# Start and end of a token-mixing kernel rearranged: who copies chunk 0 out of PSUM, where chunk 1 is convolved, the order of the last two steps

## The chip, the cores and the metric

The kernel runs on one core of a Trainium2 chip. The metric is device time of one execution in microseconds (us). Engines are named as the profile names them: PE (TensorE, matrix products), DVE (VectorE), ACT (ScalarE), POOL (GpSimd), SP (SyncE). SP and POOL each feed a queue of transfers (DMA); what stands in a queue is issued strictly in order.

## The reference

Input `x` is 8 batches x 4224 tokens x 192 channels, fp32.

```python
w = softmax(weight)                       # 8 head groups x 7 taps
x = causal depthwise convolution(x, w)    # the 24 channels of a head group share their taps
theta = x @ w_theta                       # 192 x 192
zr, zi = x * cos(theta), x * sin(theta)
y = w_tok_r @ zr + w_tok_i @ zi           # along the tokens, 4224 x 4224 each
u = x + y
out = u + relu(u @ w_ch)                  # 192 x 192
```

The two products along the tokens are almost all of the arithmetic.

## The kernel before

**Tiles.** The 4224 tokens are cut in 33 chunks of 128, each made of 32 tokens from each quarter of the sequence. A row of a tile is a token; its 1536 columns are 8 batches x 192 channels. Output tokens are in 33 blocks of 128, taken in pairs (17 units). Data are fp16 for PE, sums fp32.

**Chunk.** `Chunk.__init__` loads the tokens (four transfers by POOL, L199, into `xw`) and copies the 16 tokens of history before each quarter out of the chunk before (four transfers by SP, L190, `xw<-xw`). `conv(j)` convolves half of the channels on PE with band matrices (L212, into PSUM tile `pc`) and `evacuate` copies the result as fp16 into `z` (L150 on DVE or L152 on ACT). `conv_batches(g)` (L237) does it for chunk 0 alone, by halves of the batches, with two copies each: one on ACT, one on DVE. `store` writes x to DRAM (L259, SP). `transpose` turns it on PE (`tp`, L166) and copies it to `uT`. `theta(g)` multiplies with w_theta (PE, `v`, L142) and takes cosine and sine as two Sin on ACT (L287), for half of the batches. `product` multiplies by x on DVE (L293); `sums` forms differences (L302).

**Step.** There are 58 steps, each for one unit of output blocks and the chunks that are at hand then: two in step 0, growing to 11. `load_w` loads token weights (POOL, L369) into one of two `st` buffers, `turn` transposes them on DVE in 32x32 squares (L382, `wt`), `wsum` forms sums of weights (L394). A pair of blocks needs seven products in place of eight (`runs`, a Strassen scheme); steps 0 and 1 use the plain eight. `mix` (L500) issues the matmuls (L513, into `y`) and inserts other work at given places; `give` (L448) adds a finished `y` to `pv` (DVE, L456; in the first round ACT copies, L454). Rounds one and two keep `pv` in DRAM (`part`, L526). In the last steps (53 to 57: 9, 7, 6, 4 and 2 chunks) `outputs` makes the result: `cast` of `pv` to fp16 (`ub`), `turn_u` (PE `tp`, then `uT`), `output` (PE `v` with w_ch, then DVE L546 and the store L551). The last step has a single block.

**Buffers.** PSUM: two for `pc`, `tp`, `v` (pool `mmps`), two for `y` (pool `yps`). `xw` and most `pv` share six buffers called "big"; `z` has eleven.

**Order.** Each engine executes in program order (`in_order`), so order in the source is order on the chip. At the start the source writes the order out by hand: chunk 0, then a loop over chunks 1 to 12 in which `between(n)` inserts up to n pairs of `y` matmuls whose chunks are ready. `idle(n)` issues n matmuls of zeros (`noise`, L671): eight in front of the taps' matmuls (`bp`, L705), the others in gaps of the start. `step_events` (L584) places the tasks of a step at times from 0 to 7, 7 being its end.

Of the kernel before, what the change touches and what calls it, by code (L numbers as in the profile page):

```python
# [10 lines left out]
ALU = mybir.AluOpType  # L11
F16 = mybir.dt.float16
# [4 lines left out]
def kernel(  # L17
# [70 lines left out]
    def dve(ins):  # L88
        return in_order("dve", ins)
# [34 lines left out]
    wth = constp.tile([P, 4, D], F16, name="wth")  # L124
    wch = constp.tile([P, 4, D], F16, name="wch")

    def channel_pieces(w):

        return ((slice(0, P), 0, w[0:P, :]), (slice(0, R), 1, w[P:D, :]),
                (slice(R, P), 2, w[0:R, :]), (slice(0, P), 3, w[R:D, :]))  # L130
# [27 lines left out]

        act(nc.scalar.dma_start(out=uT, in_=u, transpose=True))

    def transposed(uT, u, gs, by_dve=False):

        tp = banks("tp", F16)
        for g in gs:
            for k in range(6):
                pe(nc.tensor.transpose(  # L166
                    tp[:, g, k * P : (k + 1) * P],
                    u[:, g * GC + k * P : g * GC + (k + 1) * P], ident,
                ))
        g = slice(gs[0], gs[-1] + 1)  # L170
        evacuate(
            uT[:, :, :].rearrange("p (g k) s -> p g (k s)", g=NG)[:, g, :],
            tp[:, g, 0 : 6 * P], by_dve,
        )
# [4 lines left out]
    class Chunk:  # L179
# [21 lines left out]
                    in_=x[:, t0 : t0 + n, :].rearrange("b s d -> s b d"),  # L201
                )

        def conv(self, j):

            if j == 0:
                self.z = zpool.tile([P, 7, HN], F16, name="z", tag="z")
                self.x = self.z[:, T2 : T2 + 2, :].rearrange("p t n -> p (t n)")
            pc = banks("pc")
            for h in range(4):  # L210
                for half in range(2):
                    pe(nc.tensor.matmul(  # L212
                        pc[half * 2 * Q : (half + 1) * 2 * Q, h // 2,
                           h % 2 * B * G : (h % 2 + 1) * B * G],
                        lhsT=bands[:, 4 * j + h, :, :].rearrange("p a m -> p (a m)"),
                        rhs=self.xw[:, half, :, (4 * j + h) * G : (4 * j + h + 1) * G],
                        start=True, stop=True,
                    ))
            evacuate(
                self.x.rearrange("p (b d) -> p b d", d=D)[  # L220
                    :, :, 4 * j * G : 4 * (j + 1) * G
                ].rearrange("p b (i h g) -> p i h b g", i=2, h=2),
                pc[:, :, 0 : 2 * B * G].rearrange("p i (h b g) -> p i h b g", h=2, b=B),
                self.k == 1 or (self.k in (2, 3) and j == 1),
            )
            if j == 1:
                self.store()

        def conv_batches(self, g):

            if g == 0:
                self.z = zpool.tile([P, 7, HN], F16, name="z", tag="z")
                self.x = self.z[:, T2 : T2 + 2, :].rearrange("p t n -> p (t n)")
            pc = banks("pc")
            for h in range(H):
                for half in range(2):
                    pe(nc.tensor.matmul(  # L237
                        pc[half * 2 * Q : (half + 1) * 2 * Q, h // 4,
                           h % 4 * GB * G : (h % 4 + 1) * GB * G],
                        lhsT=bands[:, h, :, :].rearrange("p a m -> p (a m)"),  # L240
                        rhs=self.xw[:, half, g * GB : (g + 1) * GB, h * G : (h + 1) * G],
                        start=True, stop=True,
                    ))
            for i in range(2):
                evacuate(
                    self.x.rearrange("p (b d) -> p b d", d=D)[
                        :, g * GB : (g + 1) * GB, 4 * i * G : 4 * (i + 1) * G
                    ].rearrange("p b (h g) -> p h b g", h=4),
                    pc[:, i, 0 : 4 * GB * G].rearrange("p (h b g) -> p h b g", h=4, b=GB),
                    i == 1,  # L250
                )
            if g == NG - 1:
                self.store()
# [17 lines left out]
        def transpose_batches(self, g):  # L271
            if g == 0:
                self.xT = turned()
            transposed(self.xT, self.x, [g], True)

        def theta(self, g):
            v = channel_mix(self.xT[:, 6 * g : 6 * g + 6, :], wth).rearrange(
# [52 lines left out]
    class Step:  # L330


        def __init__(self, t):
# [18 lines left out]
                    self.ahead.append((i, 2 * NU - NW + 2 * (t % NU) if far else start[-1],  # L352
                                       (t // NU - 1 - far) % 2))
            self.plain = self.first and self.pair and self.n <= NP
            self.time = 0.324 * self.n * (8 if self.plain else 7 if self.pair else 4)
            self.st, self.w, self.xr, self.ub, self.uT, self.pv = {}, {}, {}, {}, {}, []

        def known(self, tb):
# [99 lines left out]
        def runs(self):  # L458


            if self.pair:
                return [
                    ("11", Z11, "c1", True, (0, 0, True)),
                    ("S1", T1, "c2", True, (1, 1, True)),
                    ("S2", T2, "c1", False, (0, 1, True)),
                    ("S4", Z22, "c2", False, (0, 1, False)),
                    ("S3", T3, "c1", False, (1, 1, False)),
                    ("12", Z21, "c3", True, (0, 0, False)),
                    ("22", T4, "c1", False, (1, 0, True)),
                ]  # L470
            return [
                ("11", Z11, "c1", True, (0, 1, True)),
                ("11", T1, "c2", True, None),
                ("12", Z21, "c1", False, (0, 0, True)),
                ("12", Z22, "c2", False, (0, 1, False)),
            ]
# [23 lines left out]
        def mix(self, events):  # L500
# [23 lines left out]
            if not self.final:  # L524
                for i, tb in enumerate(self.tbs):
                    nc.sync.dma_start(  # L526
                        out=part[(self.t // NU) % 2][tb, :, :], in_=self.pv[i]
                    )

        def cast(self, i, g):  # L530
            if g == 0:
                self.ub[i] = wk.tile([P, N], F16, name="ub", tag="ub", bufs=2)
                self.uT[i] = turned()
            cols = slice(g * GC, (g + 1) * GC)
            evacuate(self.ub[i][:, cols], self.pv[i][:, cols], self.t >= NSTEP - 2 and g == 0)

        def turn_u(self, i, g):
            transposed(self.uT[i], self.ub[i], [g])

        def cross_u(self, i):  # L540
            crossed(self.uT[i], self.ub[i])

        def output(self, i, g):
            u = self.pv[i][:, g * GC : (g + 1) * GC]
            ub = u.rearrange("p (k n) -> p k n", k=2)
            dve(nc.vector.scalar_tensor_tensor(  # L546
                out=ub, in0=channel_mix(self.uT[i][:, 6 * g : 6 * g + 6, :], wch), scalar=0.0, in1=ub,
                op0=ALU.max, op1=ALU.add,
            ))
            rows = slice(self.tbs[i] * P, (self.tbs[i] + 1) * P)  # L550
            nc.sync.dma_start(  # L551
                out=out[g * GB : (g + 1) * GB, rows, :].rearrange("b s d -> s b d"),
                in_=u.rearrange("p (b d) -> p b d", d=D),
            )

        def outputs(self):

            found = []
            for i in range(len(self.tbs)):
                if not self.late:  # L560
                    at = 1 if i or not self.pair else 0.9 - self.time / 7
# [13 lines left out]
            return found  # L575

    steps = [Step(t) for t in range(NSTEP)]
    NPS = max(s.t for s in steps if s.plain)
    outputs = [
        (sum(s.time for s in steps[: t + 1]) + at, f)  # L580
# [3 lines left out]
    def step_events(t):  # L584
        found = []
        s = steps[t]
        if t + 1 < NSTEP:
            found += steps[t + 1].w_tasks()
            found.append((1.6, steps[t + 1].load_rows))
            for i in steps[t + 1].adds:  # L590
                found.append((2 + 2 * i, lambda i=i: steps[t + 1].load_x(i)))
                found.append((3.6 + 2 * i, lambda i=i: steps[t + 1].add_x(i)))
# [106 lines left out]
    ))  # L699
    taps = constp.tile([KS, H], F16, name="taps")  # L700
    dve(nc.vector.tensor_tensor(out=taps, in0=wcol, in1=wsum[0:KS, :], op=ALU.mult))
    idle(8)
    bp = banks("bp")
    for q in range(Q):
        pe(nc.tensor.matmul(  # L705
# [31 lines left out]

    steps[0].load_rows()
    steps[0].load_w(1)
    load_chunk(2)  # L740
    steps[0].load_w(2)
    load_chunk(3)
    for m in (1, 2):
        steps[1].load_w(m)
    load_chunk(4)
    load_chunk(5)
    for g in range(NG):
        chunks[0].conv_batches(g)
    idle(2)
    for g in range(NG):  # L750
        chunks[0].transpose_batches(g)
    for i in range(1, NW + 2):
        ch = chunks.get(i) if i < NW else None
        old = chunks[i - 1] if i <= NW else None

        def between(n):
            left = more(n)
            if i < 3:
                idle(min(left, 2) if i == 1 else 0)

        if ch:
            ch.conv(0)
        between(2)
        if old:
            old.theta(0)
        ready[0] = i - 2
        between(1)
        if ch:
            ch.conv(1)
        between(2)  # L770
        if old:
            old.theta(1)
        if i in (1, 3):
            for name in ("11", "21"):
                steps[i // 2].turn(name)
        if i + 3 < NW:
            load_chunk(i + 3)
        between(1)
        if i == 1:
            for first in (Z11, Z21):  # L780
                old.product(first, slice(0, 1))
        if ch:
            ch.transpose()
        if i == 1:
            for first in (Z11, Z21):
                old.product(first, slice(1, 2))
        elif old:
            old.product(Z11)
        between(2)
        if i > 1 and old:  # L790
            old.product(Z21)
        if i in (1, 3):
            for name in ("12", "22"):
                steps[i // 2].turn(name)
        between(1)
        if old and start[i - 1] > NPS:
            old.sums(0)
# [38 lines left out]
```

## Time and profile before

| | us |
|---|---|
| median of three runs | 1437.17 (1436.29 to 1440.14) |
| the profiled execution | 1437.24 |
| its span (first to last instruction) | 1435.4 |
| PE busy | 1410.6 (98%) |
| DVE busy | 973.8 (68%) |
| POOL busy | 434.4 (30%) |
| ACT busy | 310.8 (22%) |

The profile is of one execution. "Busy" is time in which an engine executes; the issuing of transfers is not counted on SP. "Idle before, releaser" is the gap ahead of an instruction and what ended it. The chain of waits runs back from the last instruction and gives 90% of its length to PE. TensorE's granted clock had a mean of 0.999 of full speed.

### The profile page before, as it was taken

Reading aid. Unit: us, or ns where it says so; the run is one execution under the profiler, and the core shown is the slowest. Engines: PE = TensorE matmul, PEld = TensorE weight load, DVE = VectorE, ACT = ScalarE, POOL = GpSimd, SP = SyncE. Lnnn points to the kernel's source line nnn. Section 1 sums busy time; section 2 is a strip of 40 time slices with the busy share of each in tenths; the row PEclk is TensorE's granted clock in tenths of the full one; section 3 lists DMA queues with packets and bytes.
Section 4 is the critical chain, followed back from the end, with each engine's and each line's share of the span. In section 5 each row is a group of like instructions: output and inputs, shape, how many; then the busy total and the mean of one; then the engine's idle time right before and its main releaser. Section 6 shows DMA issues by size and latency. Waiting matters only on the chain.

```text
span 1435.4 us, 23761 instructions
## 1 busy us (share of the span) xinstructions
PE 1410.6 (98%) x9825; PEld 890.3 (62%) x9825; DVE 973.8 (68%) x1046; ACT 310.8 (22%) x374; POOL 434.4 (30%) x655
## 2 busy tenths in 40 slices
PE   8899999999999999999999999999999999999997
PEld 5556666666666666666666666666566666666665
DVE  6893554545548787866666657877777677767686
ACT  5951101111124254000000004435100110010133
POOL 8511211111233332532433343233324123213120
PEclk9999999999999999999999999999999999999999
DMA  9975766564699999898899989989999999999884
GB/s 187 241 162 134 147 122 131 97 151 91 145 232 227 232 237 234 214 258 176 227 242 223 236 149 247 235 194 258 257 212 205 218 205 217 204 195 199 167 204 146
DMA packets 272028, 281.98 MB, mean 196 GB/s; under 512 B 106672, under 2 KB 240176, under 8 KB 271920
## 3 DMA queue, kind: packets, MB, share of 16 engines
q0 software_dynamic: 162464, 92.15, 48.5%
q1 hardware_dynamic: 71824, 178.88, 35.2%
q10 hardware_dynamic: 37632, 9.44, 4.6%
q8 instruction: 77, 1.26, 0.4%
q14 instruction: 31, 0.25, 0.1%
HBM read 245.49 MB, written 108.13 MB: 246 GB/s over the span
## 4 chain that ended last, share of the span: by engine, by line
PE 90%; DMA 5%; DVE 2%; ACT 1%; POOL 1%; issue 1%; DVEq 0%; ACTq 0%; POOLq 0%; SPq 0%
PE y L513 81%; PE v L142 5%; DMA xw<-in_x_dram 2%; DMA st<-in_moe_w_tok_r_dram 2%; PE tp L166 1%; PE pc L212 1%; ACT z L287 1%; DVE wt L382 1%; POOL st L369 1%; DVE pv L456 1%; DVE pv L546 0%; POOL xw L199 0%; DMA xw<-xw 0%; DMA st<-in_moe_w_tok_i_dram 0%; DMA wsb<-in_weight_dram 0%
## 5 line engine op out<-in xcount | busy, mean ns | idle before, releaser
L513 PE MATMUL y<-z,wt 128*128 128x384 f16 x7668 | 1281.9, 326 | 4.9 <-DVE pv L456 3.7
L513 PEld LDWEIGHTS <-wt 128*128 128x128 f16 x7668 | 743.6, 98 | 481.9 <-issue 5.6
L456 DVE TENSOR_TENSOR pv<-y,pv 128x768 f32<-128x768 f32 x318 | 303.3, 954 | 321.4 <-PE y L513 281.3
L382 DVE STREAM_TRANSPOSE wt<-st 128x1408 f16<-128x1408 f16 (+7 forms) x224 | 327.4, 1465 | 50.1 <-PE y L513 36.2
L369 POOL DMA_DIRECT2D st<-in_moe_w_tok_r_dram x232 | 132.3, 578 | 459.8 <-DVE wt L382 448.7
L369 POOL DMA_DIRECT2D st<-in_moe_w_tok_i_dram x232 | 132.5, 579 | 407.0 <-DVE wt L382 398.3
L394 DVE TENSOR_TENSOR wt<-wt 128x1408 f16<-128x1408 f16 (+6 forms) x208 | 173.3, 833 | 40.2 <-PE y L513 38.0
L152 ACT ACTIVATE z<-pc 128x768 f16<-128x768 f32 (+1 forms) x62 | 47.5, 803 | 385.6 <-PE pc L212 381.3
L152 ACT ACTIVATE ub<-pv 128x768 f16<-128x768 f32 x63 | 50.2, 835 | 334.1 <-DVE pv L456 305.3
L454 ACT ACTIVATE pv<-y 128x768 f32<-128x768 f32 x66 | 53.7, 814 | 280.4 <-PE y L513 280.4
L142 PEld LDWEIGHTS <-uT 128*128 128x128 f16 x1056 | 91.2, 98 | 24.6 <-issue 8.0
L434 POOL TENSOR_TENSOR pv<-pv,xr 128x1536 f32<-128x1536 f32 x24 | 74.4, 3102 | 66.7 <-DVE pv L546 21.9
L199 POOL DMA_DIRECT2D xw<-in_x_dram x132 | 76.3, 587 | 26.3 <-ACT pv L454 5.2
L546 DVE SCALAR_TENSOR_TENSOR pv<-v,pv 128x768 f32<-128x768 f32 x66 | 62.9, 954 | 27.5 <-PE v L142 27.0
L302 DVE TENSOR_TENSOR z<-z 128x768 f16<-128x768 f16 x132 | 71.2, 553 | 2.2
L287 ACT ACTIVATE z<-v,half_pi 128x768 f16<-128x768 f32 x66 | 59.7, 904 | 57.8 <-PE v L142 57.1
L152 ACT ACTIVATE uT<-tp 128x1536 f16<-128x1536 f16 (+1 forms) x47 | 56.7, 1209 | 56.9 <-PE tp L166 56.9
L293 DVE TENSOR_TENSOR z<-z 128x1536 f16<-128x1536 f16 (+1 forms) x68 | 60.6, 926 | 4.2 <-ACT z L287 4.2
L142 PE MATMUL v<-wth,uT 128*128 128x192 f16 x528 | 55.0, 248 | 2.7 <-ACT z L287 2.2
L142 PE MATMUL v<-wch,uT 128*128 128x192 f16 x528 | 54.2, 246 | 2.1 <-DVE pv L546 1.2
L287 ACT ACTIVATE z<-v 128x768 f16<-128x768 f32 x66 | 53.3, 807 | 0.0
L212 PE MATMUL pc<-xw,bands 96*64 96x192 f16 x512 | 30.5, 253 | 4.0 <-DMA xw<-xw 3.3
(45 smaller groups left out, 145.0 us busy)
## 6 DMA issues: line engine op xcount, KB each, us to landing
part<-pv SPq DMA_DIRECT2D x79, 768.0 KB, 4.2
pv<-part SPq DMA_DIRECT2D x79, 768.0 KB, 6.0
out_dram<-pv SPq DMA_DIRECT2D x66, 384.0 KB, 4.6
st<-in_moe_w_tok_r_dram POOLq DMA_DIRECT2D x136, 176.0 KB, 5.8
st<-in_moe_w_tok_i_dram POOLq DMA_DIRECT2D x136, 176.0 KB, 5.3
xs<-z SPq DMA_DIRECT2D x132, 96.0 KB, 5.0
xw<-in_x_dram POOLq DMA_DIRECT2D x121, 96.0 KB, 6.4
xr<-xs SPq DMA_DIRECT2D x24, 384.0 KB, 4.5
```

Of the source, the lines that this page charges most:

```text
L142: pe(nc.tensor.matmul(v[:, k, b * D : (b + 1) * D], lhsT=tT[:, 3 * k + b + i, :], rhs=w[:, 2 * b + i, :], start=(i == 0), stop=(i == 1),))
L152: act(nc.scalar.activation(out=out, in_=in_, func=AT.Copy))
L199: nc.gpsimd.dma_start(out=self.xw[lo : lo + n, h, :, :], in_=x[:, t0 : t0 + n, :].rearrange("b s d -> s b d"),)
L287: act(nc.scalar.activation(**args))
L302: dve(nc.vector.tensor_tensor(out=z[:, o, :], in0=z[:, a, :], in1=z[:, b, :], op=ALU.subtract))
L369: pool(nc.gpsimd.dma_start(out=st[a * Q : (a + 1) * Q, 0:nb, :, 0:n] .rearrange("i r bt s -> i (r bt) s"), in_=w[self.tbs[0] * P : (self.t ...
L382: dve(nc.vector.transpose(self.w[name][:, 0 : self.n, :, :], self.st[int(name[1])][:, int(name[0]) - 1, :, 0 : self.n * Q] .rearrange("p b ...
L394: dve(nc.vector.tensor_tensor(out=self.w[name][:, 0 : self.n, :, :], in0=self.w[a][:, 0 : self.n, :, :], in1=self.w[b][:, 0 : self.n, :, : ...
L434: ins = pool(nc.gpsimd.tensor_tensor(out=self.pv[i], in0=self.pv[i], in1=self.xr[i], op=ALU.add))
L456: dve(nc.vector.tensor_tensor(out=o, in0=yv, in1=o, op=ALU.add))
L513: pe(nc.tensor.matmul(y[cn][:, q, 0:BH], lhsT=self.w[wn][:, c, :, :].rearrange("p bt i -> p (bt i)"), rhs=chunks[k].z[:, zn, q * BH : (q + ...
L546: dve(nc.vector.scalar_tensor_tensor(out=ub, in0=channel_mix(self.uT[i][:, 6 * g : 6 * g + 6, :], wch), scalar=0.0, in1=ub, op0=ALU.max, o ...
```

## The change

- `conv_batches`: the two copies of a half of chunk 0 are cut by batches, no longer by channels; each reads both PSUM banks.
- `transpose_batches`: the second half of `uT` of chunk 0 is copied by ACT in place of DVE.
- The start is written out for chunks 0 and 1: theta(0) and theta(1) of chunk 0 follow each other with only the convolutions of chunk 1 between them. These are put in the PSUM buffers of `y` (`loose`). All other `idle` matmuls of the start go, except two; in front of the taps there are 12 in place of 8.
- The second weight load of step 0 is issued before the load of chunk 2. The four `turn`s of step 0 come in the order 11, 12, 21, 22 (before: 11, 21, 12, 22), and the second digit tells the `st` buffer that is read (1: w_tok_r, 2: w_tok_i).
- In the loop, one pair of `y` matmuls is moved from after the transposition to before theta(1).
- `load_rows` (takes the buffers of a step's sums) is at 6.9 in place of 1.6 in steps 1 to 15.
- Step 56 (`closing`) takes its seven products in another order and has its output tasks at other places. Step 57 does five runs in place of four, two for one half of its sum and then three for the other; its `ub` is cast in halves of the head's channels, the first by ACT before the second half is summed; `tp` uses a `y` buffer; the last output is made and stored in two parts.

The diff, without blank context:

```diff
...
+    def loose(name, dtype=F32):
+        return ypool.tile([P, 2, PC if dtype == F32 else 2 * PC], dtype,
+                          name=name, tag="y")
     def channel_pieces(w):
...
...
-    def transposed(uT, u, gs, by_dve=False):
-        tp = banks("tp", F16)
+    def transposed(uT, u, gs, by_dve=False, tp=None):
+        tp = banks("tp", F16) if tp is None else tp
         for g in gs:
...
...
-        def conv(self, j):
+        def conv(self, j, pc=None):
...
                 self.x = self.z[:, T2 : T2 + 2, :].rearrange("p t n -> p (t n)")
-            pc = banks("pc")
+            pc = banks("pc") if pc is None else pc
             for h in range(4):
...
...
             for i in range(2):
+                b0, nb = g * GB + i * GB // 2, GB // 2
                 evacuate(
-                    self.x.rearrange("p (b d) -> p b d", d=D)[
-                        :, g * GB : (g + 1) * GB, 4 * i * G : 4 * (i + 1) * G
-                    ].rearrange("p b (h g) -> p h b g", h=4),
-                    pc[:, i, 0 : 4 * GB * G].rearrange("p (h b g) -> p h b g", h=4, b=GB),
+                    self.x.rearrange("p (b d) -> p b d", d=D)[:, b0 : b0 + nb, :]
+                    .rearrange("p b (i h g) -> p i h b g", i=2, h=4),
+                    pc[:, :, 0 : 4 * GB * G].rearrange(
+                        "p i (h b g) -> p i h b g", h=4, b=GB
+                    )[:, :, :, i * nb : (i + 1) * nb, :],
                     i == 1,
...
...
                 self.xT = turned()
-            transposed(self.xT, self.x, [g], True)
+            transposed(self.xT, self.x, [g], g == 0)
...
...
             self.plain = self.first and self.pair and self.n <= NP
-            self.time = 0.324 * self.n * (8 if self.plain else 7 if self.pair else 4)
+            self.time = 0.324 * self.n * (8 if self.plain else 7 if self.pair else 5 if self.n <= 2 else 4)
+            self.closing = False
             self.st, self.w, self.xr, self.ub, self.uT, self.pv = {}, {}, {}, {}, {}, []
...
...
+            if self.closing:
+                return [
+                    ("12", Z21, "c2", True, (0, 0, False)),
+                    ("11", Z11, "c1", True, (0, 0, False)),
+                    ("S1", T1, "c3", True, (1, 1, False)),
+                    ("S2", T2, "c1", False, (0, 1, False)),
+                    ("S4", Z22, "c3", False, (0, 1, False)),
+                    ("S3", T3, "c1", False, (1, 1, False)),
+                    ("22", T4, "c1", False, (1, 0, False)),
+                ]
             if self.pair:
...
...
                     ("22", T4, "c1", False, (1, 0, True)),
+                ]
+            if self.n <= 2:
+                return [
+                    ("12", Z21, "c1", True, None),
+                    ("11", Z11, "c1", False, (0, 0, False)),
+                    ("11", Z11, "c2", True, None),
+                    ("11", T1, "c2", False, None),
+                    ("12", Z22, "c2", False, (0, 1, False)),
                 ]
...
...
+        def cast_half(self, i, h, gs, by_dve):
+            if i not in self.ub:
+                self.ub[i] = wk.tile([P, N], F16, name="ub", tag="ub", bufs=2)
+                self.uT[i] = turned()
+            bs = slice(gs.start * GB, gs.stop * GB)
+            o, u = (
+                v[:, :].rearrange("p (b h e) -> p b h e", h=2, e=HD)[:, bs, h, :]
+                for v in (self.ub[i], self.pv[i])
+            )
+            evacuate(o, u, by_dve)
         def cast(self, i, g):
...
             cols = slice(g * GC, (g + 1) * GC)
-            evacuate(self.ub[i][:, cols], self.pv[i][:, cols], self.t >= NSTEP - 2 and g == 0)
-        def turn_u(self, i, g):
-            transposed(self.uT[i], self.ub[i], [g])
+            evacuate(self.ub[i][:, cols], self.pv[i][:, cols], self.t >= NSTEP - 2 and g == 1)
+        def turn_u(self, i, g, by_dve=False, tp=None):
+            transposed(self.uT[i], self.ub[i], [g], by_dve, tp)
...
-        def output(self, i, g):
+        def output(self, i, g, parts=1):
             u = self.pv[i][:, g * GC : (g + 1) * GC]
             ub = u.rearrange("p (k n) -> p k n", k=2)
-            dve(nc.vector.scalar_tensor_tensor(
-                out=ub, in0=channel_mix(self.uT[i][:, 6 * g : 6 * g + 6, :], wch), scalar=0.0, in1=ub,
-                op0=ALU.max, op1=ALU.add,
-            ))
+            v = channel_mix(self.uT[i][:, 6 * g : 6 * g + 6, :], wch)
             rows = slice(self.tbs[i] * P, (self.tbs[i] + 1) * P)
-            nc.sync.dma_start(
-                out=out[g * GB : (g + 1) * GB, rows, :].rearrange("b s d -> s b d"),
-                in_=u.rearrange("p (b d) -> p b d", d=D),
-            )
+            for j in range(parts):
+                ks = slice(2 * j // parts, 2 * (j + 1) // parts)
+                dve(nc.vector.scalar_tensor_tensor(
+                    out=ub[:, ks, :], in0=v[:, ks, :], scalar=0.0, in1=ub[:, ks, :],
+                    op0=ALU.max, op1=ALU.add,
+                ))
+                b0, nb = g * GB + GB * j // parts, GB // parts
+                nc.sync.dma_start(
+                    out=out[b0 : b0 + nb, rows, :].rearrange("b s d -> s b d"),
+                    in_=u.rearrange("p (b d) -> p b d", d=D)[
+                        :, GB * j // parts : GB * j // parts + nb, :
+                    ],
+                )
...
             found = []
+            if self.closing:
+                edge = -self.time / 7 - 1e-6
+                for g in range(NG):
+                    found.append((edge - 1.2 + 0.1 * g, lambda g=g: self.cast(0, g)))
+                    found.append((edge + 1e-7 * g, lambda g=g: self.turn_u(0, g)))
+                    found.append((-0.3 + 0.6 * g, lambda g=g: self.output(0, g)))
+                    found.append((0.25 + 0.1 * g, lambda g=g: self.cast(1, g)))
+                    found.append((1.95 + 0.65 * g, lambda g=g: self.turn_u(1, g)))
+                    found.append((3.2415 + 0.07 * g, lambda g=g: self.output(1, g)))
+                return found
+            if self.n <= 2:
+                found.append((-1.6, lambda: self.cast_half(0, 0, slice(0, NG), False)))
+                found.append((0.001, lambda: self.cast_half(0, 1, slice(0, NG), True)))
+                for g in range(NG):
+                    found.append((0.01, lambda g=g: self.turn_u(
+                        0, g, False, loose("tp", F16))))
+                    found.append((0.3 + 0.1 * g, lambda g=g: self.output(0, g, 1 + g)))
+                return found
             for i in range(len(self.tbs)):
...
...
     steps = [Step(t) for t in range(NSTEP)]
+    steps[-2].closing = True
     NPS = max(s.t for s in steps if s.plain)
...
...
             found += steps[t + 1].w_tasks()
-            found.append((1.6, steps[t + 1].load_rows))
+            found.append((6.9 if 0 < t < NU - 1 else 1.6, steps[t + 1].load_rows))
             for i in steps[t + 1].adds:
...
...
     dve(nc.vector.tensor_tensor(out=taps, in0=wcol, in1=wsum[0:KS, :], op=ALU.mult))
-    idle(8)
+    idle(12)
     bp = banks("bp")
...
...
     steps[0].load_w(1)
+    steps[0].load_w(2)
     load_chunk(2)
-    steps[0].load_w(2)
     load_chunk(3)
...
     load_chunk(5)
+    c0, c1 = chunks[0], chunks[1]
     for g in range(NG):
-        chunks[0].conv_batches(g)
+        c0.conv_batches(g)
     idle(2)
     for g in range(NG):
-        chunks[0].transpose_batches(g)
-    for i in range(1, NW + 2):
+        c0.transpose_batches(g)
+    c0.theta(0)
+    c1.conv(0, loose("pc"))
+    c0.theta(1)
+    c0.product(Z11, slice(0, 1))
+    c1.conv(1, loose("pc"))
+    steps[0].turn("11")
+    for g in range(NG):
+        c1.transpose_batches(g)
+    c0.product(Z21, slice(0, 1))
+    for first in (Z11, Z21):
+        c0.product(first, slice(1, 2))
+    for name in ("12", "21", "22"):
+        steps[0].turn(name)
+    load_chunk(4)
+    ready[0] = 0
+    for i in range(2, NW + 2):
         ch = chunks.get(i) if i < NW else None
         old = chunks[i - 1] if i <= NW else None
-        def between(n):
-            left = more(n)
-            if i < 3:
-                idle(min(left, 2) if i == 1 else 0)
+        between = more
+        if i == 2:
+            old.theta(0)
+            between(2)
         if ch:
...
         between(2)
-        if old:
+        if old and i > 2:
             old.theta(0)
...
             ch.conv(1)
-        between(2)
+        between(3)
         if old:
             old.theta(1)
-        if i in (1, 3):
+        if i == 3:
             for name in ("11", "21"):
-                steps[i // 2].turn(name)
+                steps[1].turn(name)
         if i + 3 < NW:
...
         between(1)
-        if i == 1:
-            for first in (Z11, Z21):
-                old.product(first, slice(0, 1))
         if ch:
             ch.transpose()
-        if i == 1:
-            for first in (Z11, Z21):
-                old.product(first, slice(1, 2))
-        elif old:
+        if old:
             old.product(Z11)
-        between(2)
-        if i > 1 and old:
+        between(1)
+        if old:
             old.product(Z21)
-        if i in (1, 3):
+        if i == 3:
             for name in ("12", "22"):
-                steps[i // 2].turn(name)
+                steps[1].turn(name)
         between(1)
...
```

## Prediction

> **What bounds the kernel now.** I read the page first: PE is busy for 98% of the span, and the chain of waits gives PE 90%, so time can only come from where PE stands still, or from a slower clock. The second view cuts the span at places where the character changes; its columns are the stretch, its length, the busy time of PE, PE's weight loads, DVE, ACT and POOL (instructions in brackets), the granted clock, the DMA share and GB/s.
>
> ```profile
> 0.00:26.00 26.00, 19.81 (x202) 14.07 (x203) 14.70 (x33) 11.17 (x15) 22.11 (x49) 1.00 1.20 165
> 26.00:70.00 44.00, 40.92 (x385) 26.81 (x384) 35.25 (x56) 40.26 (x51) 25.04 (x44) 1.00 1.26 241
> 70.00:80.00 10.00, 7.30 (x59) 5.02 (x60) 9.90 (x16) 5.38 (x7) 1.79 (x5) 0.83 1.01 214
> 80.00:102.00 22.00, 19.86 (x154) 12.58 (x152) 20.22 (x27) 13.79 (x17) 3.36 (x6) 1.00 0.73 162
> 102.00:940.00 838.00, 838.00 (x5580) 517.56 (x5579) 534.70 (x540) 140.00 (x163) 253.21 (x376) 1.00 0.83 189
> ...
> 1400.00:1420.00 20.00, 18.86 (x148) 12.43 (x146) 14.65 (x19) 7.78 (x10) 0.83 (x2) 1.00 0.49 140
> 1420.00:1436.00 16.00, 7.65 (x83) 5.92 (x81) 7.94 (x9) 5.41 (x7) 0.00 (x0) 0.95 0.44 149
> ```
>
> From 102 to 940 us PE never stops, and the change leaves the order of the work there as it is. What it can reach is the idle time of PE at the start, 6.2 + 3.1 + 2.7 + 2.1 = 14.1 us, and at the end, 1.1 + 8.4 = 9.5 us. Part of the start is not idle in truth: the `noise` matmuls (21 of L671) count as busy.
>
> The third view, the timeline, shows what ends the idle time at the start.
>
> ```profile
> 11.38 1.20 DVE L150 CAST z<-pc 128x384 f16<-128x384 f32 x2 [0.87 <-ACT z L152]
> 15.71 0.90 ACT L287 ACTIVATE z<-v,half_pi 128x768 f16<-128x768 f32 x1 [3.73 <-PE v L142]
> 18.22 0.90 ACT L287 ACTIVATE z<-v,half_pi 128x768 f16<-128x768 f32 x1 [0.91 <-PE v L142]
> 18.33 2.28 POOL L369 DMA_DIRECT2D st<-in_moe_w_tok_r_dram  x4 [1.44 <-DVE wt L382]
> 25.43 0.59 PE L212 MATMUL pc<-xw,bands 96*64 96x192 f16 x8 [0.69 <-DMA xw<-xw]
> 40.46 0.49 PE L212 MATMUL pc<-xw,bands 96*64 96x192 f16 x7 [0.65 <-DMA xw<-in_x_dram]
> 71.59 0.24 PE L212 MATMUL pc<-xw,bands 96*64 96x192 f16 x1 [1.61 <-DMA xw<-xw]
> ```
>
> Chunk 0's two pairs of Sin stand 0.91 us apart, but the convolutions of chunks 3, 5 and 9 wait for transfers, and from 26 to 70 us ACT is busy 40.26 of 44 us (92%). The last waits of the start are thus on DMA and ACT, not on chunk 0.
>
> **Chunk 0's copies.** The split by batches leaves the DVE copy of each half behind the ACT copy of the same half, because both write one tile; the row at 11.38 (0.87 us of waiting on ACT) stays. I take 0; bounds -0.87 (both overlap) and +0.1. Chunk 0's second `uT` copy goes from DVE (half of the 1.20 us at 12.88) to ACT (0.81 us by the same copy at the end of the kernel), beside the first: 0.
>
> **Chunk 0's theta.** theta(0) begins behind the transpositions (they end at 13.48) and not at 14.79. It runs before 14.60, where the trace has PE at half pitch (noise 0.320 us each before it, 0.163 after), so it takes 1.43 us (the eight of L142 at 74.80, in another half-speed stretch) and not 0.82. The first Sin begins at 15.0, and four of about 0.85 end at 18.4 where they ended at 19.82: 1.4 us earlier. Who gets it? Next on PE is chunk 2. Its load is issued at 12.34 and not at 10.07, since w_i (2.28 us of POOL) now stands ahead of it; SP's history copies of chunk 3 wait for that load, and the row at 25.43 already waits 0.69 us for them. Going through PE's order with these durations, chunk 2 is transposed at 24.8 (before 24.6, 23.91 + 0.83) and chunk 3 begins at 25.5 (before 25.43). So the 1.4 us is lost again: 0, bounds -1.4 and +0.7.
>
> **Weights of step 0.** Transposition 21 is third, ending near 21.3 (DVE does the copies and products of chunk 0 ahead of it), and it frees the buffer for w_r of step 1. That load is issued at 21.4, not 18.33: 3.1 us later. Behind it in POOL's queue are w_i (then at 23.65, before 21.93) and chunks 4 and 5 (25.9, before 24.19): 1.7 us later. Chunk 4's four loads landed by 31.51; PE reaches chunk 4 at about 31.95 (32.11 before). With the full 1.7 us it lands at 33.2 and PE stands for 1.25 us; with the lag of the loads at 14.61 (5.0 us for the last) in place of this row's 5.6 us, at 32.6 and PE stands 0.65. I take +0.9. Then chunk 5: PE waited 0.65 + 0.65 us there for the histories, which SP issued from 32.10 behind the `part` store at 31.67. The change puts ACT's two copies of step 0 (1.61 us at 30.83) ahead of chunk 2's second Sin pair; the store goes out at about 30.3, and a PE that comes later finds the histories landed: -1.1. The sum from 26 to 42 us is -0.2 (bounds -0.9 and +1.2).
>
> **Other steps of the start.** Seven noise matmuls fewer (21 to 14, 0.33 us each): they stood in gaps, 0. The `y` pair moved ahead of theta(1) makes ACT wait 0.33 us at most for a Sin pair that is behind others on ACT: 0. `load_rows` at 6.9 gives the same buffers with the same waits: 0; no transfer is issued by it in these steps. The wait of 1.6 + 1.0 us at chunk 9 (71.59) and the clock of 0.83 in that row, together 3.7 to 4.6 us, hang on POOL's load of chunk 8 behind weights that wait for DVE; nothing of that is reordered, and I leave it.
>
> **The clock.** From 72.63 to 76.04, 3.41 us, PE ran at half pitch after the 3.41 us before it had PE busy for 29%; stretches with 59 to 64% kept full pitch. Between 14.6 and 21.4 the changed order has PE busy for 55 to 58%, near the upper row: I take no drop; one drop costs 3.41/2 = 1.7 us. The Trainium skill ("TensorE: Matmul & The Clock Gate", section "What's actually happening") says that the array falls to half clock after an idle window and needs about 3.4 us of busy time to come back, which speaks against taking fillers away. By that rule one lost window would make this sum 1.7 us larger. The twelve fillers in front end at 6.25 and not at 5.15, next to the taps at 6.54. By the same rule the clock could then be full from 7.8 and the first Sin 0.9 us earlier; the sum would still end at chunk 3's histories.
>
> **The end.** Before, the last `y` ended at 1420.75 and six outputs followed:
>
> ```profile
> 1424.77 1.94 DVE L546 SCALAR_TENSOR_TENSOR pv<-v,pv 128x768 f32<-128x768 f32 x2 [0.44 <-PE v L142]
> 1427.68 0.96 DVE L546 SCALAR_TENSOR_TENSOR pv<-v,pv 128x768 f32<-128x768 f32 x1 [0.98 <-PE v L142]
> 1428.69 1.52 PE L142 MATMUL v<-wch,uT 128*128 128x192 f16 x16 [0.22 <-DVE pv L546]
> 1429.55 1.82 DVE L546 SCALAR_TENSOR_TENSOR pv<-v,pv 128x768 f32<-128x768 f32 x2 [0.91 <-PE v L142]
> ```
>
> DVE ends at 1431.37, waiting 0.98 and 0.91 us for PE. After, four `y` matmuls more (4 x 0.163 = 0.65 us), and two outputs and all of step 56's transpositions stand among the last products; walking through the waits from 1403 us, the last `y` ends at 1424.06. Then: last sum 0.95, cast of one half on DVE 0.55, first transpositions 0.49, two `uT` copies on ACT 2 x 0.81, `v` 0.82: 1428.5. DVE has finished the output before it at 1429.3 and does the last in two of 0.5 us: 1430.35, 1.0 us earlier. The last store is half as large; the stores of 384 KB took 2.65 us, I take 0.3 off. Together -1.3; bounds -2.4 (all three DVE waits gone, 0.44 + 0.98 + 0.91) and +0.6 (the matmuls unhidden).
>
> **Sum.** -0.2 - 1.3 = -1.5 on 1437.24, which is 0.07 above the median: 1435.7. A measurement of this kernel can tell 0.3%, 4.3 us: faster is below 1432.9, slower above 1441.5.
>
> **Rivals.** (a) The wait at chunk 9 goes, because the front reaches it in another phase: -3.7 to -4.6 more, 1431.1 to 1432.0. For it: it is a matter of 1.6 us between two queues. Against: both sides move together. (b) Slower: the load of w_r behind the third transposition. If its 3.07 us reach chunk 4 in full, that lands at 34.58, and PE stands 2.63 us, as long as in the hole of 70 to 73 us (2.57), and pays its half-clock window: 2.63 + 1.71 = 4.34; chunk 5's 1.3 us wait may be absorbed. With the end: 1439.0 to 1440.3; 1441.6 if the end gains nothing, 1442.0 if a second window (1.71) is lost. It decides from a landing of chunk 4 later than 34.5. For it: POOL then has nothing to issue from 16.9 to 21.4. Against: DMA is over 100% by its share, with 5 us of lag, which a hole shortens. (c) Nothing is gained at either side: the end stays bound by DVE and its stores, 1437.
>
> **How the numbers follow.** Forecast 0.46, (a) 0.27, (b) 0.17, (c) 0.10. Of (a) 0.24 is under 1432.9, of the forecast 0.03 (its bounds reach -3.3): faster 0.27. Of (b) 0.07 is over 1441.5, and 0.05 of the forecast, where the upper bounds meet two lost clock windows (+1.2 + 0.6 + 3.4 = +5.2, 1442.4): slower 0.12. Same 0.61. The range reaches to (a)'s lower end and (b)'s middle: 1430.8 to 1440.8.
>
> **What would show it.** Right: Sins of chunk 0 from 15.0, step 1's w_r at 21.4, a short wait at chunk 4, none at chunk 5, the same hole with clock 0.83 at 70 to 76, last DVE 1 us earlier. Wrong: no hole at 70 us (a), a clock under 1 between 14 and 40 us (b), or any difference between 102 and 1400 us.

## The result

| | median us | runs | mean granted clock |
|---|---|---|---|
| before | 1438.03 (1434.83 to 1440.32) | 22 | 0.998 (35 later runs) |
| the change | 1440.93 (1436.10 to 1444.07) | 22 | 0.996 |

The ratio is 1.0020, interval 1.0012 to 1.0028: 2.9 us slower, where 1.5 us faster was forecast, and just above the range. The profiled execution of the change does not show it. It took 1436.10 us (span 1434.0), the shortest of the 22. Comparing one profile with one profile would have confirmed the forecast (1436.10 against 1437.24) and been wrong. Its stretches, same columns as before:

```profile
0.00:26.00 26.00, 19.45 (x204) 12.68 (x204) 14.45 (x33) 13.72 (x19) 21.98 (x49) 0.93 1.18 161
26.00:70.00 44.00, 39.73 (x376) 26.23 (x375) 34.44 (x55) 39.85 (x50) 25.16 (x45) 1.00 1.29 253
70.00:80.00 10.00, 7.94 (x63) 5.38 (x64) 9.93 (x16) 4.82 (x7) 2.20 (x4) 0.83 1.04 201
80.00:102.00 22.00, 19.38 (x152) 12.39 (x151) 20.29 (x28) 13.18 (x16) 2.96 (x7) 1.00 0.69 149
...
1420.00:1436.00 16.00, 7.45 (x74) 5.32 (x71) 7.54 (x11) 3.93 (x6) 0.00 (x0) 0.91 0.44 150
```

The clock column counts the time ahead of the first recorded clock change as full. Before's 1.00 for the first row hides the half pitch until 14.60; the change's 0.93 is one window at half speed (9.89 to 13.30) that follows one at full speed (from 6.47). So the two first rows, and the means of kernels with eight and with twelve fillers in front, are not to be set against each other.

And single instructions from its timeline (start, duration, engine, line, what):

```profile
13.51 0.90 ACT L293 ACTIVATE z<-v,half_pi 128x768 f16<-128x768 f32 x1 [0.73 <-PE v L146]
...
19.73 2.28 POOL L376 DMA_DIRECT2D st<-in_moe_w_tok_r_dram  x4 [2.88 <-DVE wt L389]
...
31.88 0.52 PE L216 MATMUL pc<-xw,bands 96*64 96x192 f16 x7 [0.88 <-DMA xw<-in_x_dram]
...
77.11 0.48 PE L538 MATMUL y<-z,wt 128*128 128x384 f16 x2 [1.44 <-DVE pv L463]
...
1426.68 2.89 DVE L587 SCALAR_TENSOR_TENSOR pv<-v,pv 128x768 f32<-128x768 f32 x4 [0.73 <-PE v L146]
```

The first Sin of chunk 0 starts 2.2 us earlier (15.71 before), step 1's first weights go out 1.4 us later (18.33), chunk 4 waits 0.88 us for its load, and at 77 us PE waits for DVE, where the profile before has no wait. At the end DVE finishes without the gaps of 0.98 and 0.91 us. From product 7501 of the mix to the end of the span it takes 52.14 us (before 53.02): 0.88 us gained, and 0.9 us in every trace with this end.

### The profile page after: what moved, and what is told of

The parts are those of the page before. It is cut to its first block, busy times and chain, and to the rows that moved or that the text cites. A ratio compares the mean times of both kernels' runs of the same rounds, so it can differ in the third digit from the quotient of the medians.

```text
span 1434.0 us, 23761 instructions
## 1 busy us (share of the span) xinstructions
PE 1409.1 (98%) x9822; PEld 888.5 (62%) x9822; DVE 972.0 (68%) x1045; ACT 311.6 (22%) x376; POOL 434.2 (30%) x655
## 4 chain that ended last, share of the span: by engine, by line
PE 92%; DVE 3%; DMA 2%; ACT 1%; issue 1%; POOL 1%; SPq 0%; DVEq 0%; ACTq 0%
PE y L538 83%; PE v L146 5%; PE tp L170 2%; PE pc L216 1%; DMA xw<-in_x_dram 1%; POOL st L376 1%; DVE pv L463 1%; ACT z L293 1%; DVE z L308 1%; DVE z L299 0%; DMA st<-in_moe_w_tok_r_dram 0%; DVE wt L389 0%; DMA xw<-xw 0%; DMA st<-in_moe_w_tok_i_dram 0%; DVE pv L587 0%
## 5 line engine op out<-in xcount | busy, mean ns | idle before, releaser
L587 DVE SCALAR_TENSOR_TENSOR pv<-v,pv 128x768 f32<-128x768 f32 (+1 forms) x67 | 62.9, 942 | 24.9 <-PE v L146 24.5
```

Of the source, the lines that this page charges most:

```text
L587: dve(nc.vector.scalar_tensor_tensor(out=ub[:, ks, :], in0=v[:, ks, :], scalar=0.0, in1=ub[:, ks, :], op0=ALU.max, op1=ALU.add,))
```

## The experiments

First, which end of the kernel loses, and four suspects. **A**: the clock, which falls to half in more executions because noise matmuls are gone or moved. **B**: POOL's queue (step 0's second weights ahead of chunk 2; step 1's weights behind the third transposition). **C**: the new end. **D** came with the second set: the pair of products ahead of theta(1).

**e1_start**: the change's start, before's end. (The text on record says that `load_rows` is as before; in the kernel that ran it is at 6.9, as in the change.)

```diff
 the change, but:
-    steps[-2].closing = True          (and step 57's runs, casts, outputs as before)
```

> The start of the change with the end of before (and load_rows as before). The change measured 2.9 us slower than before in the median, while its one profile is 1.1 us faster than before's. Theory A (the clock: with fewer fillers and more holes the start falls to half clock in more executions, 1.7 us for each window): all of it is here, +3 to +5 us, mean clock lower than before's. Theory B (the load of step 1's first weights behind the third transposition): +3 to +4 us as well, at an unchanged clock, with a wait for chunk 4 of over 1 us in the trace. Theory C (the new end is the slow part): 0 to -1 us.

1440.96, ratio 1.0026 (1.0013 to 1.0039). The whole loss is here, +3.7 us. PE waits 1.47 and 0.89 us for chunk 4's load in its trace, as B asked; but A had asked for the same time, and this run does not separate the two.

**e2_tail**: before's start, the change's end.

```diff
 before, but:
+    steps[-2].closing = True          (and step 57's runs, casts, outputs of the change)
```

> The end of the change with the start of before: closing order of step 56, five runs in step 57, half casts, last output in two parts. Theories A and B: -0.9 us (in the two profiles the stretch from the same matmul at 1395 us to the end of the span is 0.9 us shorter). Theory C: +3 to +4 us.

1436.74, ratio 0.9999 (0.9989 to 1.0009), 0.5 us under before in the median. C falls. The trace has the 0.88 us, the times cannot resolve it.

**e3_nofill**

```diff
 before, in between(n):
-                idle(min(left, 2) if i == 1 else 0)
```

> Before without the 11 noise matmuls between 14 and 20 us (eight in front and two behind chunk 0's convolution stay); the results do not depend on them. Theory A: +2 to +4 us, with half-clock windows in the first 40 us of the trace. Theories B and C: 0 (the matmuls stand in gaps).

1436.36, ratio 0.9994 (0.9984 to 1.0005). The eleven noise matmuls were worth nothing, the trace has no half-speed window between 15 and 73 us, and A in this form falls.

**e4_turn**

```diff
 the change, but:
-    for name in ("12", "21", "22"):
+    for name in ("21", "12", "22"):
```

> The change with step 0's transpositions in the order 11, 21, 12, 22 again, so that the first weight buffer is free after the second. Theory B: step 1's first load is issued 0.5 to 1 us earlier than in the change's trace (19.73), chunk 4 does not wait, 3 us faster than the change. Theories A and C: like the change within 1 us (+3 us on before).

1439.84, ratio to before 1.0018 (1.0008 to 1.0028): 1.1 us under the change by the medians, 0.3 by the ratios (1.0018 and 1.0020), not 3. The load goes out 0.55 us earlier (19.18), as asked, but chunk 4 still waits, 1.40 us. Half of B at the most.

**e5_idle12** and **e6_idle8**: the noise in front of the taps, put into before, and taken out of the change.

```diff
 before:             the change:
-    idle(8)         -    idle(12)
+    idle(12)        +    idle(8)
```

> Before with twelve noise matmuls in front of the taps in place of eight, nothing else. The slow part is in the start (start alone 1440.96, end alone 1436.74, before 1437.28). Theory A (clock: the earlier warm-up is followed by a half-speed window in the same place in which chunk 0 is turned, and windows later lie worse): +2 to +4 us. Theory B (POOL's queue) and theory D (the pair of products moved ahead): 0 to -1 us, since chunk 0's chain runs at full clock sooner.

> The change with eight noise matmuls in front of the taps, as before. Theory A: 2 to 4 us faster than the change (1437 to 1439). Theories B and D: like the change, 1440 to 1442.

1436.60, ratio 0.9997 (0.9986 to 1.0008), and 1440.84, ratio 1.0026 (1.0015 to 1.0038). A falls in this form too.

**e7_loads** and **e8_pairs**: B's edit undone, and D's.

```diff
 e7: the change, but:
+    load_chunk(2)
     steps[0].load_w(2)
-    load_chunk(2)
 ...
-    for name in ("12", "21", "22"):
+    for name in ("21", "12", "22"):
 e8: the change, but in the loop, ahead of theta(1) and behind product(Z11):
-        between(3)
+        between(2)
 ...
-        between(1)
+        between(2)
```

> The change with POOL's queue as before: chunk 2's load ahead of step 0's second weights, and step 0's transpositions in the order 11, 21, 12, 22. Theory B (loads of chunk 2 and of chunks 4 and 5 come later and DVE, which the traces show without a pause from 50 to 100 us, starts its stretch later): 3 us faster than the change, 1437 to 1438; DVE's idle time from 30 to 50 us falls from 8.6 us to before's 8.1 or less. Theories A and D: like the change, 1440 to 1442.

> The change with the pairs of products in the loop where they were before (two after conv(1), two after the first product). Theory D (the pair ahead of theta(1) delays ACT's Sin and with it DVE in every chunk): 2 to 4 us faster than the change. Theories A and B: like the change, 1440 to 1442.

1438.20, ratio 1.0004 (0.9992 to 1.0015), and 1437.53, ratio 0.9998 (0.9985 to 1.0010). Each alone gives some 3 us back (by the ratios, against the change's 1.0020: 2.3 and 3.2). e7's own trace does not show the sign that was asked of it: DVE is idle for 9.4 us from 30 to 50 us, not 8.1.

**The start by itself.** The whole kernel scatters from run to run (standard deviation 1.5 to 2.2 us), so the next kernels stop after step 5 of 58. Four to six runs of each, the median of all of them.

```diff
-        for t in range(NSTEP):
+        for t in range(6):
             yield from steps[t].mix(step_events(t))
 ...
-    for at, f in sorted(outputs, key=lambda e: e[0]):   (no outputs; one store of a raw sum)
```

> Before, cut after step 5 of 58 (the first six steps, one store of a raw sum to the output, nothing else; so everything after about 150 us is left out). A ruler for the three others: in the four traces with before's start the last product of step 5 begins at about 151 us, so some 155 to 160 us, with less spread than the whole kernel because later waits are gone.

> The change, cut in the same way. Theory E (the start itself costs nothing and its loss arises later, in the wait for weights between 940 and 1030 us that differs by 0 to 3.6 us among the traces): 0 to -1 us against the cut of before. Theories B and D (loads; pairs): +3 to +4 us already here.

> The cut change with POOL's queue and the order of step 0's transpositions as before. The whole kernel with this edit measured 1438.2 where the change has 1440.9. If B is right and the loss is in the start: 2 to 3 us less than the cut change. If E: the same as it within 1 us.

> The cut change with the pairs of products in the loop where they were before. The whole kernel with this edit measured 1437.5. If D is right and the loss is in the start: 3 us less than the cut change. If E: the same within 1 us.

158.03, 161.63, 159.43 and 159.38. The loss of 3.6 us is complete by 160 us, so E falls; B and D each hold 2.2 us of it. The change's cut has its profile at the median of its runs (161.63), so its trace stands for its runs. The profile of the cut of before is the slowest of its four (159.65), so these two traces differ by 2.0 us, not by 3.6. Timeline of the cut of before around 75 us, then of the cut change:

```profile
74.88 0.82 PE L142 MATMUL v<-wth,uT 128*128 128x192 f16 x8 [0.16 <-ACT z L287]
...
75.74 0.90 ACT L287 ACTIVATE z<-v,half_pi 128x768 f16<-128x768 f32 x1 [0.21 <-PE v L142]
...
78.89 0.80 PE L513 MATMUL y<-z,wt 128*128 128x384 f16 x2 [3.19 <-DVE pv L456]
...
88.78 1.83 DVE L293 TENSOR_TENSOR z<-z 128x1536 f16<-128x1536 f16 x2 [1.54 <-ACT z L287]
```

```profile
79.38 0.80 PE L538 MATMUL y<-z,wt 128*128 128x384 f16 x2 [4.57 <-DVE pv L463]
79.97 1.48 PE L146 MATMUL v<-wth,uT 128*128 128x192 f16 x8
...
81.49 0.90 ACT L293 ACTIVATE z<-v,half_pi 128x768 f16<-128x768 f32 x1 [6.38 <-PE v L146]
...
82.42 1.83 DVE L299 TENSOR_TENSOR z<-z 128x1536 f16<-128x1536 f16 x2 [0.71 <-ACT z L293]
...
90.45 1.83 DVE L299 TENSOR_TENSOR z<-z 128x1536 f16<-128x1536 f16 x2 [1.93 <-ACT z L293]
```

This is D. In both kernels a product waits near 79 us for DVE to empty its `y` buffer, because DVE is behind. Before, theta(1) of chunk 8 (74.88) is issued ahead of that product. (It stands behind the convolutions of chunk 9; the texts on record call it theta(1) of chunk 9.) In the change the moved pair is that product, and theta(1) stands behind it (79.97), 5.1 us later and at half clock. ACT is idle for 6.38 us in front of its Sin, and DVE, the late engine, then waits for ACT (0.71 and 1.93 us, where the cut of before has one wait of 1.54) and gets later still. The stretches show who sets the pace, and the clock (cut of before, then the cut change; three stretches each):

```profile
50.00:70.00 20.00, 18.69 (x178) 12.29 (x176) 19.73 (x34) 19.59 (x25) 9.90 (x18) 1.00 1.16 232
70.00:80.00 10.00, 5.64 (x49) 3.73 (x50) 9.90 (x16) 5.36 (x7) 1.72 (x3) 0.92 1.09 197
80.00:90.00 10.00, 9.84 (x87) 6.62 (x85) 8.39 (x12) 7.31 (x9) 2.29 (x4) 0.91 0.80 168
```

```profile
50.00:70.00 20.00, 18.79 (x177) 12.26 (x177) 19.76 (x34) 19.79 (x26) 10.69 (x19) 1.00 1.29 261
70.00:80.00 10.00, 4.25 (x36) 2.47 (x37) 9.90 (x17) 3.59 (x5) 1.86 (x4) 0.83 0.97 181
80.00:90.00 10.00, 10.00 (x90) 7.42 (x89) 7.74 (x11) 7.23 (x9) 2.28 (x4) 0.83 0.67 143
```

DVE is busy 19.7 of 20 us from 50 to 70 and 9.90 of 10 after that, in both. The clock is at half for 3.41 us in the cut of before (78.35 to 81.76) and for 6.83 us in the cut change (76.52 to 83.35).

**Both undone, and how D works.**

```diff
 f1_both, c5_both (cut): the change with the edits of e7 and of e8
 c6_one (cut): as c5, but ahead of theta(1) and behind product(Z11):
-        between(2)
+        between(1)
 ...
-        between(2)
+        between(3)
 c7_before3 (cut): before, but in the same places between(3) and between(1)
```

> The whole change with both repairs: POOL's queue and the order of step 0's transpositions as before, and the pairs of products where they were. If B (loads) and D (the pair in front of theta(1)) together are the loss: 0.5 to 1.5 us faster than before, 1436.0 to 1437.0, the gain of the end (0.9 us) and a little of the start. If something else in the start costs too: over 1438.

> The same two repairs in the kernel cut after step 5. Cuts so far: before 158.03, the change 161.63, loads repaired 159.43, pairs repaired 159.4. B and D adding up: 157.2, a little under before. One and the same cause reached from two sides: 159.4, like each alone.

> As the cut with both repairs, but with one pair of products ahead of theta(1) and three behind the first product (before 2 and 2, the change 3 and 1). D, that the pair which waits for DVE stands in front of theta(1): theta(1) of chunk 9 is issued before that wait as with two, so 0 to -0.5 us against the cut with both repairs. If it is only a matter of how much PE has in hand in general: +1 to +2 us.

> The cut of before with only the pairs moved (3 ahead of theta(1), 1 behind the first product). D alone: +1.5 to +2.5 us on the cut of before (158.03), 159.5 to 160.5; in the trace theta(1) of chunk 9 stands behind the matmul that waits for DVE near 79 us, and ACT is idle for over 5 us in front of its Sin. If the pairs cost only together with the other edits of the start: 158.0.

f1 is the version that beats both, before only just: 1436.96 where before had 1438.19 on the same chip, ratio 0.9986 (0.9972 to 0.9999), 4.9 us under the change's ratio. c5 took 156.77. With the four cuts of the change:

| cut, us | loads as before | loads of the change |
|---|---|---|
| pairs as before | 156.77 | 159.38 |
| pairs of the change | 159.43 | 161.63 |

D costs 2.7 and 2.3, B 2.6 and 2.2, both 4.9; what is left of the start gains 1.3 on before's 158.03. Sum: -1.3 + 4.9 = 3.6. These are medians of 4 to 6 runs, and c5 ran on another chip than the four cuts before it (before's whole kernel had 1438.19 there and 1437.71 here). Resampled from their runs, the 4.9 lies between 3.9 and 5.9 (95%), each of the four costs between 0.4 and 4.2, the gain of 1.3 between 0.6 and 3.0. In c5's timeline theta(1) is ahead of the wait, and the wait is 1.03 us:

```profile
75.43 0.82 PE L146 MATMUL v<-wth,uT 128*128 128x192 f16 x8 [0.16 <-ACT z L293]
...
77.28 0.49 PE L538 MATMUL y<-z,wt 128*128 128x384 f16 x2 [1.03 <-DVE pv L463]
...
85.79 1.83 DVE L299 TENSOR_TENSOR z<-z 128x1536 f16<-128x1536 f16 x2 [0.16 <-ACT z L293]
```

c7 took 159.01: D costs 1.0 us in before's start, less than the 1.5 to 2.5 expected, and no more than the noise of these runs. Its trace has the order that was asked for, theta(1) behind the product that waits, but the wait is 0.63 us and ACT is idle for 1.01, not 5:

```profile
77.98 0.48 PE L513 MATMUL y<-z,wt 128*128 128x384 f16 x2 [0.63 <-DVE pv L456]
...
78.31 0.82 PE L142 MATMUL v<-wth,uT 128*128 128x192 f16 x8
...
79.17 0.90 ACT L287 ACTIVATE z<-v,half_pi 128x768 f16<-128x768 f32 x1 [1.01 <-PE v L142]
```

c6 took 159.18, 2.4 us over c5 where 0 to -0.5 was expected: theta(1) still further forward does not help. The moved pairs take DVE's additions with them, and in c6's trace DVE waits 2.07 us for one Sin at 85.67, then the clock falls to half at 101.32. So the place of the pair is bounded from both sides; why one is as bad as three is not settled by one trace.

D's mark is in the traces of all twenty kernels. From theta(0) to theta(1) of chunk 8 it takes 2.5 to 3.2 us in the eleven traces with two pairs ahead of theta(1), and 3.8 to 8.0 in the eight with three (2.5 in c6, with one). PE's last wait for DVE, near 101 us, is 1.83 us in each of the eleven and 2.15 in each of the eight (2.69 in c6).

**The halves of B.**

```diff
 c8_turn (cut): the change with e8's edit and
-    for name in ("12", "21", "22"):
+    for name in ("21", "12", "22"):
 ...
 c9_beforeB (cut): before, but
-    load_chunk(2)
     steps[0].load_w(2)
+    load_chunk(2)
     and step 0's transpositions in the order 11 | 12, 21, 22
```

> The cut change with the pairs and the order of step 0's transpositions repaired; the second weights of step 0 still go out ahead of chunk 2. Cuts: both repairs 156.8, pairs alone 159.4. If the transposition that holds step 1's first weights is the costly half of B: 156.8. If it is chunk 2's late load: 159.4.

> The cut of before with both queue edits of the change and nothing else: second weights of step 0 ahead of chunk 2, transpositions 11, 12, 21, 22. B by itself: +1.5 to +2.5 us on the cut of before (158.0), 159.5 to 160.5, with chunk 4's convolution waiting for its load near 32 us. If B costs only where the rest of the start runs ahead: 158.

c8 took 158.00, in the middle: of B's 2.6 us the transposition is worth 1.4 and chunk 2's late load 1.2 (medians of 4 to 6 runs on three chips, uncertain by half to one microsecond each, so the halves are not told apart). c9 took 158.70: +0.7 in before's start, where 1.5 to 2.5 was expected; this is within the noise, though chunk 4 waits 1.30 us as asked. Where B's time goes is seen only over all traces. PE waits for chunk 4's load for 0.6 to 2.5 us, mean 1.5, in the seven with all of B, and for 0 to 1.1 us, mean 0.3, in the eleven without it. The longest is in c4:

```profile
33.31 0.52 PE L216 MATMUL pc<-xw,bands 96*64 96x192 f16 x7 [2.53 <-DMA xw<-in_x_dram]
```

And from 30 to 50 us DVE is idle for 8.6 to 10.2 us, mean 9.7, in the seven with all of B, and for 7.1 to 9.7 us, mean 8.4, in the eleven without it. By these means DVE comes to its unbroken stretch some 1.3 us later; the other half of B's cost is not located.

## Why the prediction was wrong

- **The end** (-1.3 forecast): right in mechanism, -0.88 in size. DVE ended 1.3 us earlier against the same product (1.0 forecast), but the halved last store took 2.62 us from issue to landing like the full one of 2.65, so its 0.3 us did not come, and from its landing to the end of the span 0.4 us more passed.
- **The start** (-0.2 forecast): +3.6. Two terms failed.
- **"The `y` pair moved ahead of theta(1) ... 0"** measured +2.3 to +2.7 in this start. I priced the pair by its length on PE and by ACT's queue; what counts is whose wait it carries. I wrote that DMA and ACT hold the last waits of the start, from a row of 44 us that gives DVE 35.25 us. Cut at 50, before's profile has DVE busy 19.72 of 20 us, and 9.90 of 10 stood in the third row I showed. With DVE late, a `y` product will wait for it whenever PE comes early, and all that PE has behind it waits too. The row of before from 50 us:

```profile
50.00:70.00 20.00, 19.08 (x182) 12.49 (x179) 19.72 (x34) 19.27 (x25) 9.94 (x18) 1.00 1.17 225
```

- **The queue edits**: a net -0.2 forecast (+0.9 at chunk 4, -1.1 at chunk 5), +2.2 to +2.6 measured. The wait at chunk 4 was there (0.88 us in the profile), step 1's weights went out at 19.73 and not at 21.4 since the whole front was earlier; and over the traces both waits moved as forecast, chunk 4's by +1.2 and chunk 5's by -0.7 in the mean (before's profile has one wait of 0.65 us at chunk 5, which I counted twice, so -1.1 could not be had there). That nets +0.5. The sum followed PE's waits alone and left out that the late data also make DVE late; what makes up the rest of B's cost stays open.
- **Chunk 0's theta, 0**: the rest of the start, this among it, gains 1.3 us once DVE is not held up. This gain I had put at nothing; which part of the rest brings it was not tested.
- **The clock**: removing fillers costs nothing (e3), as forecast. But the waits that the change makes longer took half-speed time with them, and I had priced none in the forecast. Its size is known only roughly: with twelve fillers in each, the mean granted clock is 0.9974 in f1, 0.9966 with D alone (e7), 0.9967 with B alone (e8) and 0.9961 in the change, so up to 1.9 us of the 4.9 are half speed (uncertain by half a microsecond) and the rest is not the clock. What fell with e3, e5 and e6 is that the fillers cause it. Rival (b) had the queue, the hole and the clock. Its picture is in three of the seven traces with all of B (c4, e1, e6: waits of 1.8 to 2.5 us at chunk 4, then one half-speed window), but each of these executions is faster than its kernel's median, and D's hole at 77 us, with DVE, is not in it. That its 1439.0 to 1440.3 comes close to the 1440.93 is in part luck. The Trainium skill ("TensorE: Matmul & The Clock Gate", section "What's actually happening") has the clock fall after an idle window; here a 3.41 us window with 38% of its time filled still fell (the cut change, 73.11 to 76.52).
- Its own tests: I had named a hole at 70 to 76 us "the same" as a sign of being right, and it was the same in that profile, which was the fastest of 22 executions; the lost time is in the others.

## What to carry to other kernels

Before pricing an instruction that is moved, find the engine that has no pause in that stretch, in stretches short enough that an average cannot hide it. An in-order engine that runs ahead of the late one will stop at the first instruction that needs it: put what feeds the late engine ahead of that instruction, and measure how far, since one place further ahead cost as much again here (c6). Where executions scatter by more than the effect, cut the kernel down to the stretch in doubt before explaining a single trace.

## What the runs showed of the hardware

The grid of 3.41 us windows has another phase in each execution (changes at 14.60 in the profile before, at 6.47, 9.89 and 13.30 in the one after), so a like wait costs a half-speed window in one run and none in the next: before's waits of 1.61 and 0.96 us at chunk 9 were followed by one, c9's of 1.76 and 0.51 by none. Counted over all traces up to 104 us, as products times their full-speed pitch (0.163 us for a product of `y`), apart from the first 12 us, windows filled under 0.35 were all followed by half speed, those from 0.35 to 0.39 some, and those over that none. In the profile after, the clock also fell at 9.89, behind a window in which PE counts as busy for 2.6 of 3.41 us; 1.5 us of these were the taps' matmuls of 8 columns, and without them the window is filled to about a third. That such small matmuls do not hold the clock up is a reading of this, not a test.
